# Last-block stores of 128 partitions, and four weight sums moved within a phase, in a fused linear-attention and MLP kernel

## The chip, the cores and the metric

The kernel runs on one core of one Trainium2 chip. The metric is the device time of one launch in microseconds (us): the median of three runs is 282.42 us (280.89 to 282.59). The profile is one further execution, of 280.67 us, whose traced span is 278.9 us; the 1.77 us between lie around the span.

## The reference, cut to what matters

```python
def phi(x):
    return np.where(x > 0, x, np.exp(x) - 1.0) + 1.0
q_p, k_p = (phi(q), phi(k))                       # q, k, v: (8, 8, 576, 64)
kv = np.einsum('bhsd,bhse->bhde', k_p, v)
z = np.sum(k_p, axis=2)
num = np.einsum('bhsd,bhde->bhse', q_p, kv)
den = np.einsum('bhsd,bhd->bhs', q_p, z)[..., None] + 1e-06
x = (num / den).transpose(0, 2, 1, 3).reshape(4608, 512)
h = x @ w_in                                      # (4608, 2048)
g = h * (1.0 / (1.0 + np.exp(-beta * h)))
out = g @ w_out                                   # (4608, 512), float32
```

## The kernel before

**Blocks.** There are eight batches of 576 rows, and nine MLP blocks of 512 rows. Blocks 0 to 7 take 512 rows of their batch; the last 64 rows of every batch (those with `j = J-1 = 8` in the order row = 9 g + j) are gathered in `xT_tail` and make block 8, the last one. Every block has an H phase (`h_phase`: `x @ w_in` in 16 groups `ff` of four matmuls, each followed by a Silu on ScalarE that writes `g`) and a Y phase (`g @ w_out`). Below, H2 is the H phase of block 2 and Y2 its Y phase.

**The Y phase of blocks 2 to 8** (`y_fast`) computes the product as a two-by-two scheme with seven half-size products in place of eight. VectorE makes the sums of parts of `g` (`g_diff`, `g_sums`, written to `gs`, which is shown as the tile `stage`), and, once for all blocks, the sums of parts of `w_out`: `ws[0]` to `ws[3]`, by `w_sum(k, n)`, two instructions for each `k`. `ws[0]` and `ws[2]` are made at the end of H1, `ws[1]` and `ws[3]` in H2. The product `yc` reads `ws[1]`, the second product into `yd` reads `ws[3]`; both lie in Y2.

**Order of work.** The schedule is written by hand. `at(sh, n, f)` hangs a function behind group `ff = n` of the H phase; `run(side, ff)` calls what hangs there, after that group's `silu` and, at `ff` 3, 7, 11 and 15, after `g_diff` or `g_sums`. In H2, `kv_both(3)` (the key-value matmuls of the next batch, and their copy to `kv_q`) hangs behind `ff = 1`, `numer_all(3)` behind `ff = 4`. `numer_all` issues 72 small matmuls into two single PSUM banks and two double ones; then VectorE evacuates them (`evac`: denominators, reciprocals, product, into `xs_sb`), and SyncE transposes `xs_sb` into `xT` by DMA. The single banks are of the same pool of four as the `h_ps` of the H phase, so that groups `ff = 7` and `ff = 8` wait until VectorE has read them. Each engine works in program order.

**The stores of the last block.** `y1` and `y2` are tiles of 128 partitions, two row groups and 512 columns of float32. Partition `i*64 + g` of row group `p` is row `g` of batch `2p + i` (`y1`) or `4 + 2p + i` (`y2`). `half(i)` is the upper or lower 64 partitions; each store moves one half. `y1[:, :, 0:256]` is stored early (L809), `y2` whole after the sixth product (L823), and the right half of `y1` at the very end, in two steps `p`, each after its own half of the seventh product (L834, L836).

Of the kernel before, what the change touches and what calls it, by code (L numbers as in the profile page):

```python
# [16 lines left out]
def kernel(  # L17
# [10 lines left out]
    nc = tc.nc  # L28

    B, H, S, D = q.shape  # L30
    DM = H * D
    DFF = moe_w_in.shape[1]
    P = 128
# [3 lines left out]
    J = S // G  # L37
    NT = 5
    EA = D + 1
    HM = DM // 2  # L40
# [11 lines left out]
    def bank(name, shape=None, dt=F32):  # L52
        return hps.tile(shape or [P, 512], dt, tag="h", name=name)
# [4 lines left out]
    def banks(name, shape=None, dt=F32):  # L58
        return wps.tile(shape or [P, 2, 512], dt, tag="w", name=name)
# [15 lines left out]
    y1 = consts.tile([P, 2, DM], F32, name="y1")  # L75
    y2 = consts.tile([P, 2, DM], F32, name="y2")
# [78 lines left out]
    def table(func):  # L155
        nc.scalar.activation(act0, warm[:, 0:1], func)  # L156
# [14 lines left out]
    def phi_tile(b, a):  # L171
        st[b, a] = work.tile([P, 2, J, P], BF16, tag=f"phi{a}", name=f"phi_{a}", bufs=1)
# [14 lines left out]
    def phi_part(b, a, pr):  # L187
        x = xin(b, a, pr)
        phi_exp(b, a, pr, x)
        phi_relu(b, a, pr, x)  # L190
        phi_min(b, a, pr)
# [17 lines left out]
    def half(hh):  # L209
        return slice(hh * G, (hh + 1) * G)  # L210
# [59 lines left out]
    def q_trans_dma(b):  # L270
        st[b, "qTd"] = work.tile([P, 2, 2 * J, G], BF16, tag="qT", name="qTd", bufs=1)
        for hh in range(2):
            nc.sync.dma_start_transpose(
                out=st[b, "qTd"][:, hh],
                in_=st[b, "q"][half(hh)].rearrange("p a j c -> p (a j c)"),
            )
# [8 lines left out]
    def rows_of(t):  # L285
        return P if t < NT - 1 else G
# [139 lines left out]
    def rows(b, ts):  # L426

        if b < B:
            return out[b * S : (b + 1) * S, :].rearrange("(g j) m -> g j m", j=J)[:, ts]
        return out.rearrange("(b g j) m -> g b j m", b=B, j=J)[:, ts, J - 1]  # L430

    def y_store(b, t, c0=0, c1=512):
        for i in range(2):
            nc.sync.dma_start(
                out=rows(b, slice(2 * t + i, 2 * t + i + 1))[:, 0, c0:c1],
                in_=(y1, y2)[t % 2][half(i), (t // 2) % 2, c0:c1],
            )
# [104 lines left out]
    for t in range(NT):  # L542
        n = rows_of(t)
# [144 lines left out]
    for t in range(2, 4):  # L688
        y_store(0, t)
    phi_all(2, "k", exps=False)  # L690

    if FAST:

        def wq(i, c0):
            return w_out_sb[i][:, :, c0 : c0 + HM]

        def w_sum(k, n):

            r = slice(4 * n, 4 * n + 4)
            a, b = (  # L700
                (wq(n, HM), wq(n, 0)),
                (wq(2 + n, HM), ws[0][:, r]),
                (wq(2 + n, HM), wq(n, HM)),
                (wq(2 + n, 0), ws[1][:, r]),
            )[k]
            nc.vector.tensor_sub(ws[k][:, r], a, b)


    def run(side, n):
        for f in side.get(n, ()):  # L710
            f()

    def at(side, n, *fs):
        side.setdefault(n, []).extend(fs)
# [40 lines left out]
    def y_fast(b, side):  # L755

        g = g_sb[b % 2]
        pa, pd, pc, pb = [bank(n) for n in ("ya", "yd", "yc", "yb")]

        pbs = [banks("yb")[:, 0], banks("yb")[:, 0]] if b == B else [pb, pb]  # L760

        def part(n0, half2):
            def lhs(c, p):
                t0 = half2 * HM + p * P
                return g[:, n0 + c, t0 : t0 + P]
            return lhs

        def sums(n):
            return lambda c, p: gs[n][:, c, p * P : (p + 1) * P]

        def plain(n0, c0):
            return lambda c: w_out_sb[(n0 + c) // 4][:, (n0 + c) % 4, c0 : c0 + HM]

        def wsum(n):
            return lambda c: ws[n][:, c, :]

        def product(ps, lhs, rhs, first, ts=range(2), apart=False):
            for p in ts:
                for c in range(8):
                    nc.tensor.matmul(  # L780
                        ps[:, p * HM : (p + 1) * HM], lhs(c, p), rhs(c),
                        start=(first and (p == 0 or apart) and c == 0), stop=True,
                        skip_group_check=True,
                    )

        def v3(ps):
            return ps.rearrange("p (a m) -> p a m", a=2)

        r1 = work.tile([P, 512], F32, tag="r1", name="r1", bufs=1)
        u2 = work.tile([P, 512], F32, tag="u2", name="u2", bufs=1)  # L790
        u4 = work.tile([P, 512], F32, tag="u4", name="u4", bufs=1)
        u3 = work.tile([P, 512], F32, tag="u3", name="u3", bufs=1)
        if b < B - 2:
            table(ACTF.Exp)
        product(pa, part(0, 0), plain(0, 0), True)
        nc.scalar.copy(r1, pa)
        run(side, 0)
        product(pd, sums(2), wsum(2), True)
        run(side, 1)
        product(pa, part(8, 0), plain(8, 0), False)  # L800
        nc.scalar.copy(y1[:, :, 0:HM], v3(pa))
        run(side, 2)
        product(pc, sums(1), wsum(1), True)
        nc.vector.tensor_add(u2, pc, r1)  # L804
        nc.vector.tensor_add(u3, pd, u2)  # L805
        run(side, 3)
        if b == B:
            for i in range(2):
                nc.sync.dma_start(  # L809
                    out=rows(b, slice(i, i + 3, 2))[:, :, 0:HM], in_=y1[half(i), :, 0:HM]  # L810
                )
        for p in range(2):
            product(pbs[p], sums(0), wsum(0), True, (p,), b == B)
        for p in range(2) if b == B else ():
            ps = slice(p * HM, (p + 1) * HM)
            nc.vector.tensor_add(y2[:, p, HM:DM], pbs[p][:, ps], u3[:, ps])
        if b < B:
            nc.vector.tensor_add(y2[:, :, HM:DM], v3(pb), v3(u3))  # L818
        run(side, 4)
        product(pd, part(8, 1), wsum(3), False)  # L820
        nc.vector.tensor_add(y2[:, :, 0:HM], v3(pd), v3(u2))
        for i in range(2):
            nc.sync.dma_start(out=rows(b, slice(4 + i, 4 + i + 3, 2)), in_=y2[half(i)])  # L823
        run(side, 5)
        if b < B:
            product(pb, sums(3), plain(8, HM), False)
            nc.vector.tensor_add(y1[:, :, HM:DM], v3(pb), v3(u2))
            for i in range(2):
                nc.sync.dma_start(out=rows(b, slice(i, i + 3, 2)), in_=y1[half(i)])
        else:  # L830
            for p in range(2):
                ps = slice(p * HM, (p + 1) * HM)
                product(pbs[p], sums(3), plain(8, HM), False, (p,))
                nc.vector.tensor_add(y1[:, p, HM:DM], pbs[p][:, ps], u2[:, ps])  # L834
                for i, eng in enumerate((nc.sync, nc.scalar)):
                    eng.dma_start(  # L836
                        out=rows(b, slice(i + 2 * p, i + 2 * p + 1))[:, 0, HM:DM],
                        in_=y1[half(i), p, HM:DM],
                    )
        run(side, 6)  # L840

    def next_loads(b):

        for pr in range(2):
            v_copy(nc.gpsimd, b, pr)
        if b + 1 < B:
            nc.gpsimd.tensor_copy(gate, st[b, "qTd"][:, 1, 2 * J - 1, G - 1 : G])
            load_qk(b + 1)
            load_v(b + 1)

    for b in range(1, B + 1):
        n, m = b + 1, b + 2
        sh, sy = {}, {}
        if n < B:
            at(sh, 0, lambda: next_loads(n))
            at(sh, 8 if b == 1 else 1, lambda: kv_both(n))
            at(sh, 11 if b == 1 else 4, lambda: numer_all(n))
        if b in (1, 2) and FAST:
            for k_ in ((0, 2), (1, 3))[b - 1]:
                for n_ in range(2):  # L860
                    at(sh, 15 if b == 1 else k_, lambda k_=k_, n_=n_: w_sum(k_, n_))
        if m < B:
            y = (lambda a, f: f) if b in FAST else (lambda a, f: a)
            at(sy, 0, lambda: phi_tile(m, "q"), lambda: phi_part(m, "q", 0))
            at(sy, 1, lambda: phi_part(m, "q", 1))
            at(sy, 1, lambda: q_trans_dma(m))
            at(sy, y(6, 3), lambda: phi_tile(m, "k"), lambda: phi_part(m, "k", 0))
            at(sy, y(8, 4), lambda: phi_part(m, "k", 1), lambda: table(ACTF.Silu))
        h_phase(b, xT[b % 2] if b < B else xT_tail, sh)
        (y_fast if b in FAST else y_phase)(b, sy)  # L870
# [30 lines left out]
```

## Time and profile before

| | us |
|---|---|
| median of three runs | 282.42 (280.89 to 282.59) |
| profiled execution | 280.67 |
| its span | 278.9 |
| TensorE busy in it | 267.2 (96%) |
| VectorE busy | 169.2 (61%) |
| ScalarE busy | 169.1 (61%) |
| GpSimd busy | 46.3 (17%) |

The granted TensorE clock was 0.997 in the mean. A busy share is an average over phases; which engine is late has to be read from each phase. "PEld" is the load of weights into TensorE, which runs beside the matmuls. In a timeline, `[idle before <-releaser]` is the time that the engine stood still before that piece, and what ended it; a name with a q (SPq, ACTq) is an engine's queue, in which its DMA calls are issued.

### The profile page before, as it was taken

The numbers are of one execution on the slowest core, as the hardware profiler recorded it, in microseconds if no ns is written. First come the engines' busy times: TensorE is split into PE (matmuls) and PEld (weight loads), VectorE is DVE, ScalarE is ACT, GpSimd is POOL, SyncE is SP. The second block draws the span as 40 slices with busy tenths as digits, with TensorE's granted clock in tenths as the row PEclk, the third lists the DMA queues.
The fourth block names the chain that finished last, engine by engine and source line by source line (L and its number), as shares of the span: only waits on it lengthen the run. The fifth ranks groups of instructions, "written<-read, shape, count | busy, mean of one in ns | idle before, by whom it ended". The sixth has DMA issues, their size and how long they took to land.

```text
span 278.9 us, 6374 instructions
## 1 busy us (share of the span) xinstructions
PE 267.2 (96%) x2689; PEld 167.0 (60%) x2697; DVE 169.2 (61%) x329; ACT 169.1 (61%) x231; POOL 46.3 (17%) x60
## 2 busy tenths in 40 slices
PE   6799999999999999999999999999999999999992
PEld 2475455445444487548754875487548745864681
DVE  4772485958848797568757885788572414321532
ACT  4838876975925794579457945794572076127500
POOL 5923012303043030304030303030000000000000
PEclk9999999999999999999999999999999999999998
DMA  7999999559999946994799659956430130041014
GB/s 237 248 207 351 268 373 264 142 94 180 289 150 182 300 65 101 205 293 66 105 198 284 79 97 204 280 83 98 142 75 12 35 118 0 0 101 52 0 40 113
DMA packets 49292, 42.76 MB, mean 153 GB/s; under 512 B 30816, under 2 KB 41072, under 8 KB 49264
## 3 DMA queue, kind: packets, MB, share of 16 engines
q0 software_dynamic: 13040, 23.40, 36.0%
q1 hardware_dynamic: 36032, 18.82, 33.1%
q8 instruction: 21, 0.34, 0.5%
q10 hardware_dynamic: 192, 0.14, 0.2%
q14 instruction: 7, 0.06, 0.1%
HBM read 36.71 MB, written 9.44 MB: 165 GB/s over the span
## 4 chain that ended last, share of the span: by engine, by line
PE 59%; DVE 2%; issue 0%; DVEq 0%
PE h_ps L404 30%; PE yb L780 8%; PE yd L780 8%; PE ya L780 8%; PE yc L780 4%; PE kvp L223 1%; PE nps L331 1%; DVE phi_q L175 1%; DVE r L168 0%; DVE u L804 0%; DVE y L818 0%; DVE u L805 0%; DVE y L834 0%; DVE phi_k L175 0%; DVEq L818 0%
## 5 line engine op out<-in xcount | busy, mean ns | idle before, releaser
L412 ACT ACTIVATE g<-h_ps,beta_c 128x512 bf16<-128x512 f32 x144 | 97.8, 688 | 68.7 <-PE h_ps L404 68.7
L404 PE MATMUL h_ps<-xT,w_in 128*128 128x512 bf16 (+1 forms) x560 | 114.8, 361 | 0.4 <-DVE xT L241 0.2
L404 PEld LDWEIGHTS <-w_in 128*128 128x128 bf16 x624 | 57.3, 98 | 63.1 <-DVE xs_sb L346 1.1
L780 PEld LDWEIGHTS <-stage 128*128 128x128 bf16 x448 | 43.8, 98 | 5.5 <-issue 0.4
L780 PEld LDWEIGHTS <-g 128*128 128x128 bf16 x336 | 32.9, 98 | 5.4
L204 POOL CAST vaug<-vf 128x1152 bf16<-128x1152 f32 x14 | 18.8, 1372 | 83.8 <-DMA vf<-in_v_dram 83.8
L419 PE MATMUL y_ps<-w_out,g 128*128 128x512 bf16 x123 | 28.7, 379 | 0.4 <-issue 0.2
L780 PE MATMUL ya<-w_out,g 128*128 128x256 bf16 x224 | 26.7, 273 | 0.0
L718 DVE TENSOR_TENSOR stage<-g 128x1024 bf16<-128x1024 bf16 x14 | 9.6, 685 | 21.6 <-ACT g L412 21.6
L722 DVE TENSOR_TENSOR stage<-g 128x1024 bf16<-128x1024 bf16 x14 | 9.7, 692 | 20.7 <-ACT g L412 20.7
L346 DVE TENSOR_TENSOR xs_sb<-nps,rden 128x448 bf16<-128x448 f32 (+3 forms) x30 | 20.7, 689 | 1.0
L419 PEld LDWEIGHTS <-g 128*128 128x128 bf16 x128 | 12.2, 98 | 13.7
L163 ACT ACTIVATE e<-xk 128x1152 bf16<-128x1152 bf16 (+1 forms) x15 | 16.7, 1160 | 0.3 <-DMA xk<-in_k_dram 0.2
L163 ACT ACTIVATE e<-xq 128x1152 bf16<-128x1152 bf16 x14 | 15.6, 1159 | 0.0
L175 DVE TENSOR_TENSOR phi_q<-e,r 128x1152 bf16<-128x1152 bf16 x16 | 12.9, 805 | 2.9 <-ACT e L163 1.8
L156 ACT ACT_TABLE_LOAD x11 | 14.1, 1283 | 0.2
L404 PE MATMUL h_ps<-xT_tail,w_in 128*128 128x512 bf16 x62 | 13.9, 379 | 0.1
L175 DVE TENSOR_TENSOR phi_k<-e,r 128x1152 bf16<-128x1152 bf16 x16 | 12.8, 804 | 1.7 <-DVE r L168 0.5
L780 PE MATMUL yb<-w_out,stage 128*128 128x256 bf16 x112 | 13.4, 272 | 0.2 <-DVE y L818 0.2
L780 PE MATMUL yd<-ws,stage 128*128 128x256 bf16 x112 | 13.4, 273 | 0.0
L780 PE MATMUL yb<-ws,stage 128*128 128x256 bf16 x112 | 13.4, 273 | 0.0
L724 DVE TENSOR_TENSOR stage<-g,stage 128x1024 bf16<-128x1024 bf16 x14 | 13.1, 934 | 0.5
(96 smaller groups left out, 232.1 us busy)
## 6 DMA issues: line engine op xcount, KB each, us to landing
vf<-in_v_dram POOLq DMA_DIRECT2D x7, 1152.0 KB, 13.5
out_dram<-y SPq DMA_DIRECT2D x26, 256.0 KB, 3.7
xq<-in_q_dram POOLq DMA_DIRECT2D x7, 576.0 KB, 8.4
xk<-in_k_dram POOLq DMA_DIRECT2D x7, 576.0 KB, 11.4
out_dram<-y SPq DMA_DIRECT2D x18, 128.0 KB, 3.2
w_in<-in_moe_w_in_dram POOLq DMA_DIRECT2D x4, 512.0 KB, 11.5
g<-in_moe_w_out_dram POOLq DMA_DIRECT2D x2, 1024.0 KB, 17.0
stage<-in_moe_w_out_dram POOLq DMA_DIRECT2D x2, 1024.0 KB, 21.4
```

Of the source, the lines that this page charges most:

```text
L156: nc.scalar.activation(act0, warm[:, 0:1], func)
L163: nc.scalar.activation(e, x, ACTF.Exp)
L175: nc.vector.tensor_tensor(st[b, a][:, pr].rearrange("p j (h d) -> p j h d", h=2), st[b, a, pr, "e"].rearrange("p h j d -> p j h d"), st[b, ...
L204: eng.tensor_copy(vaug[b % 2][:, pr, :, :, 0:D], vf[:, 2 * pr : 2 * pr + 2].rearrange("p h j d -> p j h d"),)
L346: nc.vector.tensor_mul(xs_sb[:n, ils, v0 * D : v1 * D].rearrange("p i (u d) -> p i u d", d=D), pv[:, :, :, 0:D], rden[:, :, :, None].to_br ...
L404: nc.tensor.matmul(hp[:, c0:c1].rearrange("p (t n) -> p t n", n=P), w_in_sb[ff // 4][:, kc, (ff % 4) * P : (ff % 4 + 1) * P], xm, start=(k ...
L412: nc.scalar.activation(g_sb[b % 2][:, ff, :], hp, ACTF.Silu, scale=beta_c[:, ff : ff + 1])
L419: nc.tensor.matmul(yp[:, c0:c1], g_sb[b % 2][:, ff, t * P : (t + 1) * P], w_out_sb[i][:, c, c0:c1], start=(ff == 0), stop=(ff == FC - 1), ...
L718: nc.vector.tensor_sub(gs[2][:, c], g[:, c, 0:HM], g[:, c, HM:512])
L722: nc.vector.tensor_add(gs[0][:, c], g[:, c, HM:512], g[:, c2, HM:512])
L724: nc.vector.tensor_sub(gs[3][:, c], g[:, c2, 0:HM], gs[1][:, c])
L780: nc.tensor.matmul(ps[:, p * HM : (p + 1) * HM], lhs(c, p), rhs(c), start=(first and (p == 0 or apart) and c == 0), stop=True, skip_group_ ...
```

## The change

Of the eight stores of the last block, each pair over two halves becomes one call over 128 partitions, so that four calls remain, of the same bytes. A new function `tail_rows` gives the rows for it. The last two calls go by `p`: the first on ScalarE's queue, the second on SyncE's. In H2, the two `w_sum(1, ...)` move from behind `ff = 1` to behind `ff = 7`, and the two `w_sum(3, ...)` from behind `ff = 3` to behind `ff = 8`.

```diff
+    def tail_rows(p, n=1):
+        r = out.rearrange("(p n j) m -> n p j m", n=P, j=J)
+        return r[:, p : p + n, J - 1]
...
         if b == B:
-            for i in range(2):
-                nc.sync.dma_start(
-                    out=rows(b, slice(i, i + 3, 2))[:, :, 0:HM], in_=y1[half(i), :, 0:HM]
-                )
+            nc.sync.dma_start(out=tail_rows(0, 2)[:, :, 0:HM], in_=y1[:, :, 0:HM])
...
-        for i in range(2):
+        if b == B:
+            nc.sync.dma_start(out=tail_rows(2, 2), in_=y2)
+        for i in range(2) if b < B else ():
             nc.sync.dma_start(out=rows(b, slice(4 + i, 4 + i + 3, 2)), in_=y2[half(i)])
...
-                for i, eng in enumerate((nc.sync, nc.scalar)):
-                    eng.dma_start(
-                        out=rows(b, slice(i + 2 * p, i + 2 * p + 1))[:, 0, HM:DM],
-                        in_=y1[half(i), p, HM:DM],
-                    )
+                (nc.scalar, nc.sync)[p].dma_start(
+                    out=tail_rows(p)[:, 0, HM:DM], in_=y1[:, p, HM:DM]
+                )
...
         if b in (1, 2) and FAST:
             for k_ in ((0, 2), (1, 3))[b - 1]:
                 for n_ in range(2):
-                    at(sh, 15 if b == 1 else k_, lambda k_=k_, n_=n_: w_sum(k_, n_))
+                    at(sh, 15 if b == 1 else 7 + k_ // 2, lambda k_=k_, n_=n_: w_sum(k_, n_))
```

## The prediction

> **What bounds the kernel.** I read the page first, then the chain of work that ended last, then the timeline at the two places that the change touches, then tables of short stretches for the DMA rate.
>
> ```profile
> PE 267.2 (96%) x2689; PEld 167.0 (60%) x2697; DVE 169.2 (61%) x329; ACT 169.1 (61%) x231; POOL 46.3 (17%) x60
> ```
>
> ```profile
> 271.94 1.76 PE yb L780 x16
> 273.70 0.02 issue
> 273.72 0.42 DVE y L834
> ```
>
> TensorE (PE) works 96% of the span, and the chain (columns: start, us, what), which the view follows back to 102.18 us, is nearly all TensorE. So only two things shorten the time: a gap in TensorE's stream, or the tail behind its last matmul. The chain's last piece ends at 274.14; the span ends at 278.9. Those 4.76 us are stores and the closing steps:
>
> ```profile
> 272.69 1.25 SPq L823 DMA_DIRECT2D out_dram<-y  x2
> ...
> 273.31 1.35 ACTq L836 DMA_DIRECT2D out_dram<-y  x2
> ...
> 274.03 2.02 SPq L836 DMA_DIRECT2D out_dram<-y  x2
> ```
>
> SP's two last calls took 0.884 and 1.040 us (the line's own view) where its calls at L809 and L823 took about 0.60; the second was issued only at 275.0, 0.86 after its data were ready, because SP was busy with the first. It landed 2.8 later, at 277.8, the last of all (the four took 2.8 to 3.6). From there to the end it is 1.1 us. What the DMA engines did (last two columns: mean busy share, GB/s):
>
> ```profile
> 3.00:3.50 0.50, 0.50 (x2) 0.15 (x1) 0.00 (x0) 0.00 (x0) 0.00 (x0) 1.00 1.05 415
> ...
> 268.75:269.00 0.25, 0.25 (x5) 0.23 (x3) 0.25 (x1) 0.00 (x0) 0.00 (x0) 1.00 1.02 213
> ...
> 274.25:274.50 0.25, 0.00 (x0) 0.00 (x0) 0.00 (x0) 0.00 (x0) 0.00 (x0) 1.00 1.13 229
> ...
> 275.50:275.75 0.25, 0.00 (x0) 0.00 (x0) 0.00 (x0) 0.00 (x0) 0.00 (x0) 1.00 1.09 377
> ```
>
> The DMA engines are full from 273.9 to 277.25 (in the next quarter their share is 0.05). They move 512 KiB of `y2` and four times 64 KiB of `y1`, 786 KB, in 3.35 us: 235 GB/s. The rate is not even. L809's 64-partition stores ran at about 195 GB/s (262 KB from 268.65 to 270.0) with the engines full; so does the start of the tail; the tail's best three quarters of a microsecond (275.25 to 276.0: 283, 377, 319) come when calls of both halves are in flight. The opening loads, calls of 128 partitions on SP, ran at 382 to 415.
>
> The other place is H2, in the timeline (columns: start, us, engine, line, operation, written and read tiles):
>
> ```profile
> 86.90 1.28 DVE L706 TENSOR_TENSOR ws<-w_out,ws 128x1024 bf16<-128x1024 bf16 x2
> ...
> 88.11 0.16 DVE L344 TENSOR_SCALAR den<-nps 128x7 f32<-128x7 f32 x1
> ...
> 89.21 8.04 PE L404 MATMUL h_ps<-xT,w_in 128*128 128x512 bf16 x36 [0.17 <-DVE xs_sb L346]
> ...
> 107.94 1.91 PE L780 MATMUL yb<-w_out,stage 128*128 128x256 bf16 x16 [0.20 <-DVE y L818]
> ...
> 115.61 0.16 DVE L344 TENSOR_SCALAR den<-nps 128x7 f32<-128x7 f32 x1
> ```
>
> In H2 the numerators' matmuls begin at 86.33 and VectorE (DVE) begins to evacuate at 88.11, behind the `ws[3]` sums; TensorE then waits twice for the banks (0.17 at 89.21, and its weight load 0.42 at 90.17). In H3, which has no `w_sum`, they begin at 115.04 and 115.61, and TensorE doesn't wait. From the numerators' first matmul to the first `ya` it is 10.76 us in H2 (86.33 to 97.09), 10.32 in H3 (115.04 to 125.36) and 10.32 in H4 (142.96 to 153.28): H2 loses 0.44. The line at 107.94 is Y2, where TensorE waits 0.20 for VectorE.
>
> **The sums, part by part.** `w_sum(3)` (1.28 us for two) leaves the place ahead of `evac`. Behind `g_diff` (86.29, the next starts 0.61 later) `evac` can start at 86.90, 1.21 earlier. The products that free the two banks then end at 87.9 and 88.9 (now 89.15 and 90.11); TensorE asks for them two and three groups of 0.87 after 87.14, at 88.9 and 89.75. The stall goes whole: **-0.44**. `w_sum(1)` delays nobody now (DVE stands idle 0.76 behind it), so its move gains nothing.
>
> What hides the four sums in their new place: from `g_diff` at 86.29 to `g_sums` of the last groups at 98.01, DVE idles 0.61 (before 94.56) and 1.24 (before 98.01), 1.85 in all. `w_sum(3)` is inside this stretch already; `w_sum(1)` brings 1.28 more. That leaves 0.57, less the 0.44 by which TensorE and so the Silus come earlier: **0.13 us of cover**. Queued behind the sums on DVE are `g_sums` of both halves, the phi work and the additions of Y2, and TensorE waits for those; without cover every further tenth is lost at Y2's second `yb`, where DVE is already the later one. `ws[1]` would be ready about 94.3 and `ws[3]` about 95.6; they are read at 102.33 and 105.83.
>
> On SP's queue the `xT` transposes start 1.2 earlier (91.74 to about 90.5; SP stands idle there) and meet the load of `vf` that GpSimd's casts wait for. In H2, H3 and H4 the transposes began 6.5, 6.25 and 5.7 after the issue of `vf`, and the casts 13.3, 13.6 and 14.2 after it; so an estimate from these rows is casts nearly a microsecond or more later than 98.53. Their reader is `kv_both` at 111.5. Beside the casts, L723 and L724 took 1.52 and 1.51 each, instead of 0.69; in Y4, with later casts, L724 and an L168 took 1.62 and 1.40 instead of 0.69 and 0.45, about the same loss, and there the chain's pieces in Y4 lengthen by 0.11 in all (1.78 and 1.83 instead of 1.75). I take nothing for this. Bounds: -0.36 (Y2's surplus over Y3, 12.59 to 12.23 from `ya` to the next H phase, goes too) and +0.44 (the stall is paid back in Y2).
>
> The Trainium skill, "SBUF — State Buffer", section "Who interferes with whom", has VectorE and GpSimd share a port pair as an exclusive lock, so that a two-input sum that met the casts would wait; the 1.52 us of L723 agree, and the rule speaks against moving sums toward the casts. By it the term would still be -0.44, since the sums end near 95.6 and the casts come no sooner than 98.5; casts that came 3 us sooner would cost up to 0.83 for each sum that they met, as L723 did.
>
> Stores: L809 becomes one call instead of two, 267.39; SP stands idle 4.6 before L823, so it is worth nothing. L823 becomes one call at 272.69. A 128-partition issue on SP took 0.454 to 0.699 in the opening loads, so SP is free by 273.4 instead of 273.89. The first last store goes out on ACT at 273.31 as now, with nothing behind it. The second waits on SP for DVE's 274.14 and goes out at 274.17, 0.83 before today's last call. It can land no sooner than the data move. If the last call takes 2.8 again, it lands at 277.0, against 277.8: -0.8. By rate: 786 KB from 273.9 at 300 GB/s takes 2.6, to 276.5 instead of 277.25: -0.75. I choose 300 because it lies between the only two kinds of row (195 for 64 partitions alone, 393 for 128-partition loads) and near the 326 of the stretch with both halves in flight. I take **-0.8**. Bounds: at 393 the data end at 275.9, -1.35; at 195 they end at 277.95, +0.7.
>
> By the same page, section "Door 1", bandwidth follows the ports that a transfer's partitions reach: 64 partitions measured 196 GB/s, 128 measured 328 at 1 MiB. The 195 agrees; at 328 the term would be -0.95. Its section on two DMAs for both halves gives them only 6% over one; the 377 above disagrees, and the measurement decides: part of the gain is there already.
>
> Sum: -0.44 - 0.8 = -1.24. The profiled execution becomes 279.4 (span 277.7). It lies 1.75 under the median of the runs, which scatter over 1.7 us; I move the median by the same amount: 281.2.
>
> **Rivals.**
>
> *Only H2 gains.* Issues and bytes are rearranged but the stores stay at 235 GB/s; the data end at 277.25 as now, and the tail gives 0 to -0.2. For it: the engines are full throughout, and the bytes are equal. Against: 195 beside 326 shows that 235 is no ceiling. About 281.9.
>
> *The single call is slower.* Fast stretches in the tail come only with several calls in flight, over both halves and both queues. If one 512 KiB call streams at the 195 of a lone call and the last calls line up behind it, the data end 0.7 later; less 0.44 this is +0.26, 282.7. It decides below 235 GB/s. Against it speak the loads at 382 to 415. If H2 gains nothing either, 283.1.
>
> *More than I count.* Stores at load rate (-1.35), H2 whole (-0.44), Y2's wait gone (-0.36): -2.15, 280.3. For it: the loads' rate; against: the longest fast stretch of stores, block 7's from 250.75 to 251.5, ran at 347 (360, 361, 319), with both halves in flight.
>
> That the change doesn't do what it says I rule out: the edits are plain in the code; in the calls touched, eight stores become four.
>
> **How the numbers follow.** My forecast (-0.9 to -1.6) gets 0.55, only H2 0.2, the slower one 0.12, more 0.13. Range 279.6 to 282.7: from -2.15, less some 0.7 of the runs' scatter, to the slower rival. 1% is 2.8 us, about what a measurement can tell from no change. No case reaches it alone; scatter may carry the best case there (0.06) or the worst (0.04), and 0.90 stays within.
>
> **What would show it.** In H2: `den` 0.6 us after the numerators' first matmul, no wait of TensorE for `xs_sb`, 10.3 us to `ya`; `g_sums` of the last groups starting within 0.1 of the last Silu's end (else the cover failed); Y2 no longer than 12.6. In the tail: SP's last issue near 274.2 minus the 0.44, a DMA rate near 300 from there, and 3.9 to 4.0 us from the last VectorE piece to the end instead of 4.76. A rate of 195 or DVE late at Y2's second `yb` by more than 0.4 would make it wrong.

## The result, and the profile after

The changed kernel takes 278.75 us (median of four, 278.27 to 279.37) against 281.95 (four, one more than was shown ahead of the prediction, 280.89 to 282.59): ratio 0.9891, 95% interval 0.9852 to 0.9931. The forecast, 281.2 with a range down to 279.6, was right in direction and too small in size. Its profiled execution took 279.37 us with a span of 277.6, where the working had said 279.4 and 277.7 for the profiled execution. So the profile came out as worked out to 0.1 us, while the median fell 2.45 us below the forecast. Both facts have to be explained, and they have different causes; the first is luck, as the rows below show.

**H2 and Y2**, in the timeline of the changed kernel (start, us, engine, line, operation; in brackets the idle time before it):

```profile
86.97 0.16 DVE L344 TENSOR_SCALAR den<-nps 128x7 f32<-128x7 f32 x1
...
87.21 9.67 PE L404 MATMUL h_ps<-xT,w_in 128*128 128x512 bf16 x44
...
97.64 0.69 DVE L727 TENSOR_TENSOR stage<-g 128x1024 bf16<-128x1024 bf16 x1 [0.29 <-ACT g L412]
...
106.17 0.76 DVE L175 TENSOR_TENSOR phi_k<-e,r 128x1152 bf16<-128x1152 bf16 x1 [0.48 <-DVE r L168]
...
107.59 1.91 PE L785 MATMUL yb<-w_out,stage 128*128 128x256 bf16 x16 [0.23 <-DVE y L820]
```

The evacuation starts 0.58 after the numerators' first matmul (86.39), the 44 matmuls behind it run through without a stop, and from the numerators to `ya` it is 10.33 us instead of 10.76. The four sums are covered: VectorE still waits 0.29 for the last Silus at 97.64. In Y2 TensorE waits for VectorE as before, behind an idle gap of 0.48 ahead of the first `phi_k`; Y2 takes 12.61 us, before 12.59.

**The tail**, in the same view of the same kernel:

```profile
272.83 0.38 SPq L825 DMA_DIRECT2D out_dram<-y  x1
...
273.44 0.37 ACTq L839 DMA_DIRECT2D out_dram<-y  x1
273.86 0.42 DVE L838 TENSOR_TENSOR y<-yb,u 128x256 f32<-128x256 f32 x1 [0.45 <-PE yb L785]
274.31 0.34 SPq L839 DMA_DIRECT2D out_dram<-y  x1
```

and its DMA rate, in the table of stretches (the last three columns: granted clock, DMA share, GB/s):

```profile
273.75:274.00 0.25, 0.07 (x1) 0.00 (x0) 0.14 (x1) 0.00 (x0) 0.00 (x0) 1.00 0.96 360
274.50:274.75 0.25, 0.00 (x0) 0.00 (x0) 0.00 (x0) 0.00 (x0) 0.00 (x0) 1.00 1.06 410
275.50:275.75 0.25, 0.00 (x0) 0.00 (x0) 0.00 (x0) 0.00 (x0) 0.00 (x0) 1.00 0.99 328
```

These calls take 0.34 to 0.38 us to issue, where those of 64 partitions took 0.60 to 1.04 on SyncE and 0.48 to 0.56 on ScalarE. The bytes move at 356 GB/s on the mean (273.7 to 275.9), at 360 from the first full quarter of a microsecond on. ScalarE's last call lands 2.5 after its issue; the profile has no landing for SyncE's, the very last. From the end of the last VectorE piece (274.28) to the end of the span it is 3.3 us instead of 4.76: 1.44 gained.

These two gains, 0.43 and 1.44, would make 1.87, but the span is only 1.3 shorter. Most of what is missing went in Y5, which took 12.80 us instead of 12.24, and Y3, 12.40 instead of 12.23. In Y5 GpSimd's casts fell beside other VectorE instructions than in the profile before (184.81, that is 3.92 us after `ya`; before 1.60 after it): one `phi_q` took 1.69 instead of 0.76 and an L168 1.40 instead of 0.45, at a place where VectorE had just waited for ScalarE (0.54). So the 0.1 us between the working and this profile is a sum of two errors: the tail gave 0.64 more than its term, and 0.57 of the gains was lost, for the most part in Y phases that the working had put at nothing.

### The profile page after: what moved, and what is told of

It is laid out like the page before. It is cut to its first block, busy times and chain, and to the rows that moved or that the text cites. A ratio compares the mean times of both kernels' runs of the same rounds, so it can differ in the third digit from the quotient of the medians.

```text
span 277.6 us, 6368 instructions
## 1 busy us (share of the span) xinstructions
PE 267.3 (96%) x2689; PEld 167.2 (60%) x2697; DVE 170.5 (61%) x329; ACT 169.1 (61%) x231; POOL 46.2 (17%) x60
## 4 chain that ended last, share of the span: by engine, by line
PE 58%; DVE 2%; issue 1%; ACT 0%; DVEq 0%
PE h_ps L404 30%; PE yb L785 8%; PE yd L785 8%; PE ya L785 8%; PE yc L785 3%; PE nps L331 1%; PE kvp L223 1%; DVE phi_q L175 1%; DVE u L810 1%; DVE u L809 0%; ACT e L163 0%; DVE r L168 0%; DVE y L820 0%; DVE y L838 0%; DVE phi_k L175 0%
## 5 line engine op out<-in xcount | busy, mean ns | idle before, releaser
L175 DVE TENSOR_TENSOR phi_q<-e,r 128x1152 bf16<-128x1152 bf16 x16 | 13.8, 863 | 3.0 <-ACT e L163 1.8
L785 PE MATMUL yd<-ws,g 128*128 128x256 bf16 x112 | 13.4, 272 | 0.3 <-DVE u L810 0.3
L785 PE MATMUL yc<-ws,stage 128*128 128x256 bf16 x112 | 13.4, 273 | 0.0
## 6 DMA issues: line engine op xcount, KB each, us to landing
vf<-in_v_dram POOLq DMA_DIRECT2D x7, 1152.0 KB, 13.3
```

The source lines that it names most:

```text
L175: nc.vector.tensor_tensor(st[b, a][:, pr].rearrange("p j (h d) -> p j h d", h=2), st[b, a, pr, "e"].rearrange("p h j d -> p j h d"), st[b, ...
L785: nc.tensor.matmul(ps[:, p * HM : (p + 1) * HM], lhs(c, p), rhs(c), start=(first and (p == 0 or apart) and c == 0), stop=True, skip_group_ ...
```

## The experiments

The ratio is always to the kernel before on the same chip, with its 95% interval. The theory to begin with (T) was that the two terms add, and that the rest of the 3.2 us is scatter; the rival (R), that one of the parts is worth more than its profile shows. Later expectations state a T and an R of their own.

### One part at a time

The stores alone (`e1_tail`: the changed kernel, with the old places of `w_sum`):

```diff
-                    at(sh, 15 if b == 1 else 7 + k_ // 2, lambda k_=k_, n_=n_: w_sum(k_, n_))
+                    at(sh, 15 if b == 1 else k_, lambda k_=k_, n_=n_: w_sum(k_, n_))
```

> Only the stores are changed; w_sum stays at ff 1 and 3. Theory T (two terms that add, as the two profiles show them: the tail behind the last VectorE piece 4.76 to 3.3 us, H2 10.76 to 10.33; what the runs show beyond that is scatter from where GpSimd's casts meet VectorE): -1.4 us against the kernel before, 280.5 if that is at 281.95; in the profile 3.3 us from the last VectorE piece to the end, DMA near 365 GB/s, and H2 still 10.76 from the numerators to ya. Rival R (one of the parts is worth more in ordinary runs than in a profiled one, since the medians moved by 3.2): -2.4 or more here, or in e2.

Measured: 279.63 us, ratio 0.9953 (0.9935 to 0.9971), or -1.2 us against 280.85. The profile's TensorE ran at a clock of 0.95 from 5.5 us on, so only the tail is read from it: 3.2 us. Theory T held in size, and R is excluded; T's row on H2 can't be read from this profile.

The sums alone (`e2_sums`: the kernel before, with the new places of `w_sum`, the same line the other way round):

> Only w_sum is moved; the eight stores stay. T: -0.4 us (0 to -0.8); 10.33 us from the numerators' first matmul to ya in H2, Y2 still with a wait of 0.2 to 0.4 at its second yb, 4.76 us from the last VectorE piece to the end. R: -1.2 us or more, which would mean that the move also changes where the casts of the later blocks fall.

Measured: 280.52 us, ratio 0.9993 (0.9973 to 1.0013). H2 gained its 0.44 (10.32 us), but Y2 took 12.96 instead of 12.6, so 0.35 of it was paid back one phase later. T's mechanism held in H2; its -0.4 is neither shown nor excluded by the runs (-0.8 to +0.4); R's -1.2 is excluded. The profile shows where the gain went:

```profile
100.70 2.77 POOL L204 CAST vaug<-vf 128x1152 bf16<-128x1152 f32 x2 [13.29 <-DMA vf<-in_v_dram]
100.96 1.50 DVE L175 TENSOR_TENSOR phi_q<-e,r 128x1152 bf16<-128x1152 bf16 x1 [0.54 <-ACT e L163]
```

GpSimd's casts begin 3.7 us after `ya` (before 1.4), and the `phi_q` beside them takes 1.50 instead of 0.76.

Both kernels as controls, `e3_after` and `e4_before`, with no edit:

> The changed kernel again, on the same chip as its two halves. T: the sum of e1 and e2, -1.9 us (ratio 0.993); a Y phase of blocks 2 to 5 is 12.25 us where the casts fall beside g_sums, and up to 0.55 longer where they fall beside the phi of q, in this profile perhaps in another block than Y5. R: -3.2 (ratio 0.989).

> The kernel before, run as a kernel of its own: a second profile of it, and a ratio that must be 1. T: its span scatters by 0.5 to 2 us, and what is longer than in the first profile lies in Y phases of blocks 2 to 5, with casts beside other VectorE work. R: H2 or the tail is longer than 10.76 or 4.76 us.

Measured: `e3_after` 279.39 us, ratio 0.9953 (0.9933 to 0.9972); `e4_before` 0.9998 (0.9980 to 1.0016). The change is worth 1.3 to 1.5 us on this chip, less than the first comparison's 3.2 (R, excluded) and than T's -1.9, which was the sum of two profiles; the two parts as measured, -1.2 and -0.3, do add up to it. The tails of the two profiles are 3.3 and 4.7 us, and H2 10.32 and 10.76. Y5 was normal in `e3_after` and 12.50 in `e4_before`. Of the 0.5 us by which the span of `e4_before` was longer, 0.42 lay ahead of H2's numerators (86.75 against 86.33), where T had not looked for it. Theory T's scatter from the casts was seen, but at 0.3 to 0.55 us in one block it is too small for times from 280.0 to 282.6.

### The tail: calls, halves, or partitions

`e5_halves_at_once` keeps two calls of 64 partitions for `y2`, but sends them out side by side:

```diff
         for i in range(2):
-            nc.sync.dma_start(out=rows(b, slice(4 + i, 4 + i + 3, 2)), in_=y2[half(i)])
+            eng = nc.scalar if b == B and i else nc.sync
+            eng.dma_start(out=rows(b, slice(4 + i, 4 + i + 3, 2)), in_=y2[half(i)])
```

> On the kernel before, one edit: y2's second half goes out on ScalarE's queue at the same time as the first on SyncE's, still two calls of 64 partitions. Theory T (a store reaches the full rate when both halves of the partitions are in flight, in one call or two): 330 to 370 GB/s for y2 from the first quarter on, 3.8 to 4.1 us from the last VectorE piece to the end instead of 4.76, -0.7 us. Rival R (the single call is what counts; two calls of one half each share the rate of about 200): as before, 4.76 us and 235 GB/s, 0 us.

Measured: ratio 1.0006 (0.9985 to 1.0027), 4.66 us from the last VectorE piece (276.04) to the end. Its two calls went out at 274.59 and 274.60; the table of stretches shows what they moved:

```profile
276.00:276.25 0.25, 0.00 (x0) 0.00 (x0) 0.04 (x1) 0.00 (x0) 0.00 (x0) 1.00 1.11 229
276.25:276.50 0.25, 0.00 (x0) 0.00 (x0) 0.00 (x0) 0.00 (x0) 0.00 (x0) 1.00 0.93 188
276.50:276.75 0.25, 0.00 (x0) 0.00 (x0) 0.00 (x0) 0.00 (x0) 0.00 (x0) 1.00 1.12 205
```

The engines are full, and the rate is still about 200 GB/s. But the halves did not move together, although both calls were out by 275.4. The view of the DMA queues (packets, MB, share of the engines) shows for 275.75 to 277.00, and then for 277.25 to 278.00:

```profile
q1 hardware_dynamic: 110, 0.23, 91.4%
...
q10 hardware_dynamic: 107, 0.21, 92.8%
q1 hardware_dynamic: 25, 0.02, 6.5%
```

q10 is ScalarE's queue (in the tail of the kernel before it moves 0.13 MB, the size of ScalarE's two calls), q1 is SyncE's. So the calls went out side by side and moved one after the other: the first half at about 200 GB/s, the second, nearly alone, at about 280 (0.21 MB in 0.75 us). T's forecast fell and R's held, but two halves that do move together were not tested. The prediction's reading of the fast stretches fell too: one half is enough for one. Its own profile has the same at 275.75 to 276.00, at 319 GB/s, in rows of 2 KB, which are `y2`'s (those of `y1` are of 1 KB):

```profile
DMA packets 39, 0.08 MB, mean 319 GB/s; under 512 B 0, under 2 KB 0, under 8 KB 39
...
q1 hardware_dynamic: 39, 0.08, 115.0%
```

By 275.25 the rates of that profile's table add up to 255 KB, and the first half is 262 KB, so this is the second alone. Why the first half of a pair is slow and the second fast is open. The Trainium skill's "SBUF — State Buffer", section "Can I just issue two DMAs to hit both halves?", says that two such calls serialize and gain little (6% in its measurement); this run agrees with it, and the prediction had put a single stretch of 377 GB/s above it.

`e6_eight_calls` has as many calls as before, each over 128 partitions and half the columns (`e1_tail`, with every store cut in two):

```diff
...
-            nc.sync.dma_start(out=tail_rows(2, 2), in_=y2)
+            for c in (0, HM):
+                nc.sync.dma_start(
+                    out=tail_rows(2, 2)[:, :, c : c + HM], in_=y2[:, :, c : c + HM]
+                )
...
-                (nc.scalar, nc.sync)[p].dma_start(
-                    out=tail_rows(p)[:, 0, HM:DM], in_=y1[:, p, HM:DM]
-                )
+                for c, eng in ((HM, nc.sync), (HM + P, nc.scalar)):
+                    eng.dma_start(
+                        out=tail_rows(p)[:, 0, c : c + P], in_=y1[:, p, c : c + P]
+                    )
```

> The stores of the changed kernel, each cut by columns into two calls, so eight calls of 128 partitions and the same bytes, with w_sum where it was. T (coverage of the partitions sets the rate): near 330 GB/s, a little under the 365 of the changed kernel because the runs of one row are half as long; 3.4 to 3.9 us from the last VectorE piece to the end, -0.9 to -1.3 us. R (the number of calls, their issue and their landing, set the tail): 4.4 us or more, and -0.3 us at most.

Measured: ratio 0.9954 (0.9931 to 0.9977), a tail of 3.5 us, 322 to 348 GB/s while `y2` moves and about 280 for the shorter rows at the end. So the number of calls hardly matters (3.5 against 3.2 in `e1_tail`); how many partitions one call spans does.

`e7_y2_one_call` changes only L823 on the kernel before, to one call of 128 partitions:

> On the kernel before, only the store of y2 becomes one call; the other six stay. T: y2 moves at 360 GB/s, is gone 0.8 us sooner, and the last four calls find free engines, so that SyncE issues them in 0.6 us each and not 0.9 to 1.0: 3.7 to 4.0 us from the last VectorE piece to the end, -0.8 to -1.0 us of the 1.3 that all stores gave. R: the last calls set the end, and y2 alone gives under 0.4 us.

Measured: ratio 0.9961 (0.9937 to 0.9985), a tail of 3.6 us. The rates of its table show both kinds in one tail:

```profile
276.00:276.25 0.25, 0.00 (x0) 0.00 (x0) 0.23 (x1) 0.00 (x0) 0.00 (x0) 1.00 1.03 393
277.00:277.25 0.25, 0.00 (x0) 0.00 (x0) 0.00 (x0) 0.00 (x0) 0.00 (x0) 1.00 0.96 225
```

`y2` moves at 369 to 401 GB/s, then the halves of `y1` at 201 and 225 before they quicken. One call, `y2`'s, gives most of the change's whole gain (T, a little better than forecast).

### Where the scatter comes from

`e8_cast_on_act` takes the casts of `v` for batches 4 to 7 away from GpSimd:

```diff
...
-        for pr in range(2):
-            v_copy(nc.gpsimd, b, pr)
+        if b in (2, 3):
+            for pr in range(2):
+                v_copy(nc.gpsimd, b, pr)
...
+            if b in FAST:
+                at(sy, 4, *(lambda pr=pr: v_copy(nc.scalar, m, pr) for pr in range(2)))
```

> The changed kernel, with the casts of v for batches 4 to 7 moved from GpSimd, where they run beside VectorE in Y2 to Y5, to the end of those Y phases on ScalarE, which stands idle there for 4 us. Theory T (the casts make VectorE late in Y2, where it pays back 0.3 of H2's 0.44, and now and then in Y3 to Y5): Y2 falls from 12.6 to 12.9 us to 12.25, Y3 to Y5 are 12.23 in every profile, the runs scatter less, and the time is 0.5 to 0.9 us under that of the changed kernel, so a ratio of 0.992 to 0.994 against the kernel before. Rival R (Y2 is late for another reason, the idle 0.46 us of VectorE ahead of its first phi of k, or the casts on ScalarE delay the first Silus of the next H phase): Y2 stays at 12.6, ratio 0.9953 or worse.

Measured: 279.48 us, ratio 0.9945 (0.9916 to 0.9973), and 277.96 to 282.05, wider than before. The profile (span 276.2 us) has Y3 to Y5 at 12.23 each, as T said, but Y2 stayed at 12.60 with the idle gap ahead of `phi_k`, as R said. Taking the casts off GpSimd did not narrow the times; whether they scatter for another reason once the casts are on ScalarE, this run can't tell.

What does show in every list of times is the granted clock. Over 93 executions of the kernel before, from all the comparisons of this study, the 66 with a mean clock of 0.995 or more took 280.01 to 281.98 (median 280.78), and the 10 at 0.987 or less took 281.82 to 283.11 (median 282.39). The 17 between took 280.45 to 282.00 (median 281.06). Two profiles fell among executions at 0.987 or less, those of `e5` and `e7`. The table of stretches of `e7_y2_one_call` shows where (first columns: the stretch, its length, TensorE busy; the third from the end: the clock):

```profile
11.00:12.00 1.00, 0.16 (x6) 0.24 (x8) 0.76 (x1) 1.00 (x3) 1.00 (x2) 1.00 1.18 200
12.00:13.00 1.00, 1.00 (x37) 0.73 (x32) 0.46 (x3) 0.98 (x3) 0.78 (x2) 1.00 1.25 208
13.00:14.00 1.00, 0.89 (x23) 0.82 (x24) 0.16 (x3) 0.59 (x2) 0.47 (x1) 0.63 1.24 207
14.00:15.00 1.00, 1.00 (x19) 0.84 (x18) 0.55 (x2) 0.00 (x0) 0.27 (x1) 0.50 1.24 205
20.00:21.00 1.00, 1.00 (x17) 0.91 (x17) 0.61 (x2) 0.28 (x1) 0.00 (x0) 0.96 1.25 209
```

By the means 0.63 and 0.96 the clock is half from 13.3 to 20.1 us, after a start in which TensorE waits for data; H1 then begins at 53.47 instead of 51.62, 1.85 us late, and nothing later gives that back. In `e5` it is half from 13.6 to 20.4 (means 0.78 and 0.81). A shorter one stands in `e3_after`, whose mean clock is 0.992:

```profile
14.00:15.00 1.00, 0.87 (x19) 0.51 (x14) 0.78 (x4) 0.00 (x0) 0.05 (x1) 0.59 1.21 201
...
17.00:18.00 1.00, 1.00 (x16) 1.00 (x14) 0.97 (x4) 0.75 (x2) 0.02 (x1) 0.70 1.25 202
```

From 14.2 to 17.6 that is 3.4 us, half of the 6.8 in `e5` and `e7`. The Trainium skill, "TensorE: Matmul & The Clock Gate", Part 1, has TensorE at half clock after an idle window of about 3.4 us that runs freely, not from the kernel's start. The 0.50 agrees, and the stretches are as long as one and two such windows. That a gap brings them on is not shown: in `e2_sums` TensorE was busy for 0.79 of the microsecond from 10 to 11 and not at all from 11 to 12 (0.39 and 0.16 in `e7`), and the clock stayed at 1.00. A window whose place isn't tied to the kernel would fit that some executions fall and others don't with like gaps, but no run here shows where it lies.

`e9_warm` fills the start:

```diff
     q_half(0, 0, qtp[0])
-    idle(3)
+    idle(5)
...
+    idle(3)
     kv_first(0)
     z_sums(1)
```

> The changed kernel with five more idle matmuls between 7 and 12 us, where TensorE waits for data (two before the second half of q's transposes, three before the first key-value product). Theory T (the runs above 282 us of the kernel before are those in which a thin stretch of TensorE before 12 us brings the granted clock down to 0.5 from about 13.4 to 20 us, as in the profiles of e5 and e7, at some 1.5 us): no run of this kernel has a mean clock under 0.99, the highest lies within 1.2 us of the lowest, and the median is 0 to 0.3 us under e12's. Rival R (the clock falls for another reason): one or two runs of twelve under 0.99 as before, or 0.3 us slower for the added matmuls.

Measured: 279.33 us in six runs, none under a clock of 0.998. But `e12_after`, the same kernel without the filling, had none under 0.99 in its six either, so this settles nothing, and no time was gained over its 279.15.

### The gap in Y2

`e10_shift` asks what the idle 0.46 to 0.48 us of VectorE ahead of the first `phi_k` in Y2 waits for. It adds sixteen memsets that nobody needs:

```diff
...
+        if b == 2:
+            for _ in range(16):
+                at(sh, 2, lambda: nc.vector.memset(tiny, 0.0))
```

> The changed kernel with sixteen memsets of one column on VectorE in H2 behind ff 2, where it stands idle for 2 us; they do nothing but lengthen its stream of instructions. Theory T (VectorE's idle 0.46 us ahead of the first phi of k in Y2, which every profile of every kernel so far shows at the same instruction, sits at a fixed place of the instruction stream): the gap is gone from there and lies sixteen instructions earlier, in H2; Y2 falls from 12.6 to 12.25 us, -0.35 us. Rival R (the first phi of k waits for other work): the gap stays where it is, Y2 12.6, 0 us.

Measured: 278.90 us, ratio 0.9938 (0.9924 to 0.9952). The timeline of this kernel:

```profile
96.40 0.69 DVE L729 TENSOR_TENSOR stage<-stage,g 128x1024 bf16<-128x1024 bf16 x1 [0.46 <-DVE stage L728]
...
106.00 0.76 DVE L176 TENSOR_TENSOR phi_k<-e,r 128x1152 bf16<-128x1152 bf16 x1
```

The gap is gone from `phi_k` and stands ahead of an instruction of `g_sums` in H2, twelve busy instructions earlier (the semaphore instructions between them are not in this view). Y2 fell to 12.33 us. So the gap belongs to a place in the stream of instructions and not to any work; that it is the loading of instructions is a guess that no run here tests. One row fits it: q14, a DMA queue of the kind `instruction`, has one packet between 107 and 109 us in the changed kernel, behind the gap, and none between 99 and 100; in `e10` it is the other way round, again behind the gap.

`e11_all` puts `e8`, `e9` and `e10` together, and `e12_after` is the changed kernel once more:

> The changed kernel with e8's casts on ScalarE, e9's idle matmuls and e10's memsets together. If all three theories hold: Y2 to Y5 12.23 each, no run with a mean clock under 0.99, 278.3 us, ratio 0.990 to 0.992. If the theory of the instruction stream falls: 278.7.

> The changed kernel once more, on the same chip as e9 to e11, as their base. T: ratio 0.9945 to 0.9955 against the kernel before over all runs; among runs with a mean clock of 0.995 or more, 279.1 against 280.8. R: a ratio near the 0.989 of the first comparison.

Measured: `e12_after` 279.15 us, ratio 0.9943 (0.9925 to 0.9960). `e11_all` 280.13 us, ratio 0.9956 (0.9924 to 0.9988), which leaves out its two slowest runs. Its profile has Y2 to Y5 at 12.23 each as expected, and its best run, 277.92, is the lowest of the study, but its twelve runs go up to 283.87, six of them over 281, at clocks of 0.993 to 1.0. Something outside what its profile shows costs up to 5 us in some executions. Whether the casts on ScalarE bring it stays open; `e8` and `e11` are no improvement. `e10_shift` has the lowest median of these experiments, 0.25 us under `e12_after` on the same chip, which their overlapping intervals don't settle.

## Why the prediction was wrong

**The base: the step that failed.** The prediction worked on the profiled execution and then said "I move the median by the same amount". But the profiled execution took 280.67 and the median shown was 282.42. Later runs show executions near 280.8 at full clock, near 282.4 at 0.987 or less, and some between; where there is a profile, they differ by the half clock between 13 and 21 us. Two of the three times shown, 282.42 and 282.59, lie above all 66 runs at full clock and within those at low clock; their own clocks were not recorded, so this is inferred. All four executions of the changed kernel in the first comparison had a clock of 1.0. From 280.67 the same sum would have given 279.4 with a range down to about 277.9, and 278.75 lies in it. Among executions at 0.995 or more, the kernel before takes 280.78 (66 runs) and the changed one 278.97 (17 runs, the first comparison's four among them): -1.8 us. The other 1.2 of the first comparison's 3.2 are the base (281.95 less 280.78), and 0.2 lie between its four runs of the changed kernel (278.75) and the 17.

**The tail: right mechanism, mis-sized.** The term was -0.8; it is -1.44 in the first pair of profiles and -1.43 in `e3` against `e4`. The rate chosen was 300 GB/s, a middle between two rows; 356 was measured, nearer to the opening loads, the other calls of 128 partitions on SyncE (382 to 415). The data end 1.62 us after the last VectorE piece (275.9 less 274.28), where the working had 2.36 (276.5 less 274.14). Of these 0.74 the rate is 0.4 (2.2 us for the 786 KB instead of 2.6) and the start 0.34: the first bytes move 0.87 after L825's call instead of 1.21 after L823's, and the call itself takes 0.38 instead of 0.60. The bound worked out at 393 was -1.35. The argument for 300, that halves in flight together had reached 326, was a misreading: the trace of `e5` and that of the kernel before have 280 and 319 with one half moving. The rival of a lone slow call fell with all of it, and "only H2 gains" had it the wrong way round.

**H2: right to the hundredth, and paid back.** The stall of 0.44 went (10.33 in the first profile, 10.32 in all later ones with moved sums), and the cover of 0.13 held, with 0.29 left. The wrong entry was "I take nothing for this" about the casts. The working had them nearly a microsecond later, since the transposes meet the load of `vf`; in six profiles with moved sums they came 13.1 to 14.9 us after its issue, in five without 13.1 to 13.6. That the transposes are the reason was not tested. In four of the six they began 3.6 to 4.5 us after `ya` and met `phi_q` behind a wait for ScalarE, and there Y2 took 12.86 to 13.03; without moved sums it took 12.59 to 12.65. With the casts off GpSimd (`e8`) H2 had the same gain and Y2 took 12.60, so the casts are what takes it back. Where they do, of 0.44 some 0.3 to 0.4 came back in Y2, as the bound of +0.44 had allowed; over all runs the sums are worth 0.2 us (`e2`, its interval reaching from -0.8 to +0.4).

**Y2.** That TensorE waits there for VectorE was read rightly; that part of it is a gap fixed in the instruction stream was seen only with `e10`.

**The chances.** "Within 1%" is what the later comparisons give (0.9953 and 0.9943); the first one's 0.9891 is 1.1% and mixes the change's 0.6% with the base.

## What to carry to other kernels

A store that ends a kernel should span all 128 partitions in one call: a call of 64 that found the engines idle moved at little more than half the rate, two sent out side by side moved one after the other, and splitting by columns cost almost nothing. Before a median is moved, ask whether the profiled execution is of the same kind as the runs behind it; a gap of 1.75 us between the two was as large as the change. Work moved out of one queue's way can move others (here casts that slow VectorE down), and what these delay is part of the price.

## What the hardware showed unexpectedly

- Two calls of 64 partitions each, issued side by side from two queues, moved one after the other with the engines full: the first at 147 to 229 GB/s, the second at about 280 (`e5`). One call of 128 moved at 356 to 400 from the start. What makes the second of a pair faster is open.
- VectorE stood idle 0.46 to 0.48 us at one fixed place of its instruction stream, and the place moved with the stream (`e10`).
- The granted clock fell to 0.50 for 6.8 us (from 13.3 or 13.6, `e7` and `e5`) or 3.4 us (from 14.2, `e3_after`) in some executions and not in others. Executions of one kernel at a mean clock of 0.987 or less took some 1.6 us more (282.39 less 280.78).
